# Windowed attention and a gated MLP on one core: probabilities times values by blocks of 64 queries, one piece of PE work for one pair's product and the next pair's scores, both heads in one instruction

## The chip, the core and the metric

The kernel runs on one core of a Trainium2 chip. The metric is the time of one execution in device microseconds. It is 917.48 us at the median of three runs (916.28 to 917.65). A profiled execution of the same kernel took 917.38 us; its span from the first to the last instruction is 915.7 us.

Names of engines: PE is TensorE (PEld its weight loads), DVE is VectorE, ACT is ScalarE, POOL is GpSimd, SP is SyncE, which here only issues DMAs.

## What is computed

Eight batches, eight heads, 576 positions, 64 numbers a head, all fp32. Heads 0 to 3 see the 32 positions up to their own; heads 4 to 7 see every fourth position of the last 128. The eight heads' outputs, side by side, are the 512 columns of x for a gated MLP of 2048 hidden units.

```python
scores = scale * np.matmul(q, k.transpose(0, 1, 3, 2))
rel = pos[:, None] - pos[None, :]
mask_plain = (rel >= 0) & (rel < window)                                       # window = 32
mask_dil = (rel >= 0) & (rel < window * dilation) & (rel % dilation == 0)      # dilation = 4
scores = np.where(masks[None, :, :, :], scores, -1000000000.0)
attn = np.exp(scores - np.max(scores, axis=-1, keepdims=True))
attn = attn / (np.sum(attn, axis=-1, keepdims=True) + 1e-09)
x = np.matmul(attn, v)      # then transposed and reshaped to (8 * 576, 512)
h = x @ w_in
out = (h * (1.0 / (1.0 + np.exp(-1.702 * h)))) @ w_out
```

## The kernel before

**Pairs.** Two heads lie beside each other on 128 partitions, a pair; a batch has four pairs (`c`), 32 in all (`i`). The host sorts the positions of the dilated heads by their remainder modulo 4. A dilated window is then a plain window of 32 neighbours, too, and every query needs only keys of its own block of 32 and of the block before.

**Scores** (L290 to L304). For each block of 32 queries PE multiplies 32 queries by 64 keys, on tiles of 64 x 32 of its array (64 rows for a head, 32 columns for a place among the output partitions). The result of a head is 128 x 5 x 64, `sp`. Batches 0 and 1 have the mask added by PE itself (`masked`, an identity times the mask, L294) and do their scores head by head; from batch 2 on DVE adds the mask (L315 to L318) and both heads come in one piece.

**Softmax** (L306 to L344): maximum, subtraction, exponent, sum, reciprocal, product, for each head by itself where 320 elements a partition are concerned. Then DVE transposes blocks of 32 x 32 into `ct`.

**Spread** (L346 to L365). Eight copies take the blocks of `ct` into `bt`, keys on the partitions, 5 x 32 queries for each group of 128 keys. They are done by ACT or DVE, or by DMAs that SP issues one after the other (batch 1, and pairs 0 and 2 of batch 0, which have the second buffer `bts[1]`, laid into the end of `wol`).

**Product** (L373 to L383). For each group of 128 keys PE multiplies the values (128 x 64) by the probabilities of up to 160 queries, on tiles of 128 x 64, the two heads side by side on the output's partitions. Keys of a group touch queries of the next one, so the pieces overlap and add up in PSUM: 352 columns and 352 columns for the two halves of the queries. The output is x, transposed; ACT takes it out into `xm` (512 positions) and `xr` (the last 64), or in batch 0 ACT and DVE into `xh` and `xl`, its high and low part.

**MLP.** Weights arrive as eight-byte numbers and are decoded on the chip into a high and a low fp32r part (`decode`, L213, 32 pieces `n`, on ACT, DVE and POOL). Group `m0` to `m7` is the 512 first positions of a batch, group `r` the 64 last ones of all eight. A group has 16 ups (`hp`, 12 matmuls of 128 x 512 each, L457) and 16 downs (`acc`, 12 each, L493 to L497), with tanh, gate and split in between. While group m(b) runs on PE, attention of batch b + 1 is worked in between.

**PSUM** has eight banks: `acc0` to `acc3`, `sp0`, `sp1`, `av` and `hp`. Group m0 alternates its ups between `sp1` and `hp` (L451).

**What sets the order.** Nothing is scheduled by hand. Each step is added to a plan (`add`, L44) with its cost on each engine that may do it, an urgency, and the names that it reads and writes. `Plan.ordered` (L64) simulates the engines and gives one order; each engine then runs its instructions in that order, and a waiting instruction holds up all behind it. A step that the plan starts on PE is issued as a whole: for batches from 2 on, scores of both heads are one step (L368), which follows the product of the pair before (`"product"`, L369), and the product is another (L388). In the first 30 us PE's idle time is filled with matmuls that nobody reads (`warm`).

Of the kernel before, what the change touches and what calls it, by code (L numbers as in the profile page):

```python
# [7 lines left out]
F32 = mybir.dt.float32  # L8
# [9 lines left out]
P = 128  # L18
# [8 lines left out]
W = 64  # L27

# [88 lines left out]
def tile_windowed_attention_then_gated_mlp(  # L117
# [50 lines left out]
    zeros, ident = fixed([P, P], BF16, "zeros"), fixed([P, P], BF16, "ident")  # L168
    V.memset(zeros, 0.0)
# [22 lines left out]
    for j in range(2):  # L192
        G.memset(bts[j], 0.0)
# [17 lines left out]
    words = [fixed([P, DM], U32, f"words{j}") for j in range(3)]  # L211

    def decode(n, urgency):  # L213
# [14 lines left out]
        r = n % 3 if n < 5 else n % 5  # L228
        raw, word = cells[r], words[n % 3]
        R, E = f"cell{r}", f"words{n % 3}"  # L230
        taken = {8: ("qk1",), 9: ("qk1", "v1")}.get(n, ())
        freed = () if f < NF - 4 or n % 2 == 0 else ("bt1",)
# [11 lines left out]
        early = ("spread0.3",) if n in (1, 2) else ()  # L244
# [3 lines left out]
        add({DVE: -0.43, ACT: 1.35}, urgency, take_sign, (R,), (R + "l",))  # L248
# [3 lines left out]
            (R + "l",), (E, *freed))  # L252
        add({ACT: 0.62, DVE: -0.42}, urgency, lambda e: copy(e, hi, value), (E,), (key,))
        add({DVE: -0.70, POOL: 1.7}, urgency, lambda e: pair(e, lo, value, f32(hi), ALU.subtract), (E,), (key,))

    spare = [second.bitcast(F32).rearrange("p j n -> p (j n)"), xm.rearrange("p c n -> p (c n)"),
             xr[:, 1:].rearrange("p b c n -> p (b c n)")]

    def attention(b, c, urgency):

        i, dil = b * NC + c, c >= NC // 2
        u = {}
        z = i if b == 0 else 0 if b == 1 else i % 2
        y = (i + 1) % 2 if b < FIRST else 0
        pr, mx, sm, ct, bt = prs[i % 2], mxs[i % 2], sms[i % 2], cts[i % 2], bts[y]
        nq, nv = 2 * S, 2 * QT * D

        def load_qk(e):
            flat = temp([P, nq], F32, "qk", f"qk_{i}") if z == 0 else spare[z - 1][:, 0:nq]
            u["qk"] = flat.rearrange("p (a s) -> p a s", a=2)  # L270
            for rows in (slice(0, D), slice(D, P)) if i == 0 else (slice(0, P),):
                load(u["qk"][rows], qk[i, rows])

        def load_v(e):
            flat = temp([P, nv], F32, "v", f"v_{i}") if z == 0 else spare[z - 1][:, nq:nq + nv]
# [12 lines left out]
        masked, mine = b < FIRST, mask if dil else plain

        def scores(e, heads):  # L290
            for a in heads:
                u["sp", a] = bank([P, QT, W], places[a], f"sp_{i}_{a}")
                if masked:
                    T.matmul(u["sp", a], ident, mine, start=True, stop=False, skip_group_check=True)  # L294
            for t in range(QT):
                for a, j in [(a, j) for a in heads for j in range(min(4, S // 32 - 4 * t))]:
                    g, rows = 4 * t + j, slice(D * a, D * a + D)
                    dst, keys = u["sp", a][32 * j:32 * j + 32, t], u["qk"][rows, 1]
                    for w in (0, 32) if g == 0 else (0,):
                        n = 32 if g == 0 else W  # L300
                        at = max(32 * g - 32, 0)
                        T.matmul(dst[:, w:w + n], u["qk"][rows, 0, 32 * g:32 * g + 32], keys[:, at:at + n],  # L302
                                 start=not masked, stop=True, tile_position=(D * a, 32 * j),
                                 skip_group_check=True)  # L304

        def exponents(a):  # L306

            box, key = pr[:, a], f"{i % 2}{a}"
            held = (places[a],) if masked else ()

            def sp():
                return u["sp", a] if masked else box

            if not masked:
                for n, tiles, cost in ((P, slice(0, QT - 1), 0.35), (D, slice(QT - 1, QT), 0.15)):  # L315
                    add({DVE: cost}, urgency, lambda e, n=n, tiles=tiles: pair(
                        e, box[0:n, tiles], u["sp", a][0:n, tiles], mine[0:n, tiles], ALU.add),
                        (places[a],), (f"pr{key}",))  # L318
            add({DVE: 0.40}, urgency, lambda e: V.tensor_reduce(
                out=mx[:, a], in_=sp(), axis=AX.X, op=ALU.max), (*held, f"pr{key}"), (f"mx{key}",))  # L320
            add({DVE: 0.42}, urgency, lambda e: pair(
                e, box, sp(), mx[:, a, :, None].broadcast_to([P, QT, W]), ALU.subtract),
                (*held, f"mx{key}"), (f"pr{key}",))
            add({ACT: 0.42}, urgency, lambda e: A.activation(box, box, AF.Exp, scale=0.125), (), (f"pr{key}",))  # L324
            add({DVE: 0.40}, urgency, lambda e: V.tensor_reduce(
                out=sm[:, a], in_=box, axis=AX.X, op=ALU.add), (f"pr{key}",), (f"sm{key}",))

        def weights(hs):

            n, heads = hs.stop - hs.start, range(hs.start, hs.stop)  # L330
            sums, probs = [[f"{k}{i % 2}{a}" for a in heads] for k in ("sm", "pr")]
            for a in heads:
                exponents(a)
            add({DVE: -0.075}, urgency, lambda e: V.tensor_scalar(
                out=sm[:, hs], in0=sm[:, hs], scalar1=1.0e-9, scalar2=None, op0=ALU.add), (), sums)
            add({DVE: 0.07 + 0.03 * n}, urgency, lambda e: V.reciprocal(out=sm[:, hs], in_=sm[:, hs]), (), sums)  # L336
            for a in heads:
                add({POOL: 0.73, DVE: -0.48}, urgency, lambda e, a=a: pair(
                    e, pr[:, a], pr[:, a], sm[:, a, :, None].broadcast_to([P, QT, W]), ALU.mult),
                    sums, (f"pr{i % 2}{a}",))  # L340
            for half in (0, 1):
                add({DVE: 0.07 + 0.165 * n}, urgency, lambda e, half=half: V.transpose(  # L342
                    out=ct[:, half, hs], in_=pr[:, hs, :, 32 - 32 * half:64 - 32 * half]),
                    probs, [f"ct{i % 2}{half}{a}" for a in heads])  # L344
# [266 lines left out]
```

## Time and profile before

| what | value |
|---|---|
| median of three runs | 917.48 us |
| profiled execution | 917.38 us |
| its span | 915.7 us |
| granted clock of PE, mean | 0.996 |
| PE busy: `hp_m` (L457), three groups of 512 | 203.1, 199.8, 199.7 us |
| PE busy: scores, `qk` and `second`, 64 x 64 | 20.3 and 13.3 us |
| PE busy: product, 128 x 160, `v` and `second` | 15.6 and 14.3 us |
| ACT busy: copies into `bt`, 32 x 320 | 42.2 us, 468 ns each |
| DVE busy: copies into `bt`, 32 x 320 | 29.2 us, 317 ns each |

In a row of a group stand the line, the engine, the operation, what is written and read, the shapes and the count, and behind the bar the busy time and the mean of one. Matmuls overlap in the pipeline, so the busy times of PE add up to more than the span, and a price of a matmul is read from the distance of two starts. Rows of the timeline give start, busy time, engine, line, operation and count.

### The profile page before, as it was taken

Reading aid. Unit: us, or ns where it says so; the run is one execution under the profiler, and the core shown is the slowest. Engines: PE = TensorE matmul, PEld = TensorE weight load, DVE = VectorE, ACT = ScalarE, POOL = GpSimd, SP = SyncE. Lnnn points to the kernel's source line nnn. Section 1 sums busy time; section 2 is a strip of 40 time slices with the busy share of each in tenths; the row PEclk is TensorE's granted clock in tenths of the full one; section 3 lists DMA queues with packets and bytes.
Section 4 is the critical chain, followed back from the end, with each engine's and each line's share of the span. In section 5 each row is a group of like instructions: output and inputs, shape, how many; then the busy total and the mean of one; then the engine's idle time right before and its main releaser. Section 6 shows DMA issues by size and latency. Waiting matters only on the chain.

```text
span 915.7 us, 16236 instructions
## 1 busy us (share of the span) xinstructions
PE 902.4 (99%) x6738; PEld 726.3 (79%) x6738; DVE 514.1 (56%) x1140; ACT 329.0 (36%) x628; POOL 57.1 (6%) x60
## 2 busy tenths in 40 slices
PE   9899999999999999999999999999999999999997
PEld 4577777888888888888888888888888888888885
DVE  6888896755666546653676275645653433343332
ACT  4888894342433223331434143312431221121111
POOL 3212321000000000000000000000000000000000
PEclk9999999999999999999999999999999999999998
DMA  6645743111112003110221011200100010001002
GB/s 222 229 154 175 272 135 130 63 42 55 50 64 74 23 1 113 42 55 1 87 67 42 15 72 56 67 15 26 62 1 1 1 47 0 1 2 46 1 0 47
DMA packets 25177, 58.54 MB, mean 64 GB/s; under 512 B 6992, under 2 KB 8720, under 8 KB 25104
## 3 DMA queue, kind: packets, MB, share of 16 engines
q1 hardware_dynamic: 25104, 57.50, 19.3%
q8 instruction: 53, 0.87, 0.4%
q14 instruction: 20, 0.16, 0.1%
HBM read 46.14 MB, written 9.44 MB: 61 GB/s over the span
## 4 chain that ended last, share of the span: by engine, by line
PE 92%; ACT 2%; DMA 2%; DVE 2%; SPq 0%; issue 0%; DVEq 0%; ACTq 0%
PE hp_m L457 37%; PE acc_m L493 13%; PE acc_m L497 12%; PE acc_m L494 12%; PE hp_r L457 5%; PE av L381 4%; PE sp L302 3%; PE acc_r L497 2%; PE acc_r L493 2%; PE acc_r L494 2%; DMA qk<-qk_dram 1%; DMA cell<-wo_dram 1%; ACT cell L239 1%; SPq L360 0%; ACT cell L247 0%
## 5 line engine op out<-in xcount | busy, mean ns | idle before, releaser
L468 DVE SCALAR_TENSOR_TENSOR g_m<-g_m,hp_m 128x512 f32<-128x512 f32 x128 | 87.9, 687 | 250.6 <-ACT g_m L465 250.1
L493 PE MATMUL acc_m<-gh,woh 128*128 128x512 f32 x512 | 202.8, 396 | 1.1 <-ACT cell L247 0.4
L457 PE MATMUL hp_m<-xh,wih 128*128 128x512 f32 x512 | 203.1, 397 | 0.5 <-DVE xl L204 0.3
L457 PE MATMUL hp_m<-xh,wil 128*128 128x512 f32 x512 | 199.8, 390 | 0.0
L457 PE MATMUL hp_m<-xl,wih 128*128 128x512 f32 x512 | 199.7, 390 | 0.0
L494 PE MATMUL acc_m<-gh,wol 128*128 128x512 f32 x512 | 199.5, 390 | 0.0
L465 ACT ACTIVATE g_m<-hp_m 128x512 f32<-128x512 f32 x128 | 77.0, 602 | 301.5 <-PE hp_m L457 291.9
L497 PE MATMUL acc_m<-gl,woh 128*128 128x512 f32 x512 | 143.1, 392 | 0.0
L493 PEld LDWEIGHTS acc_m<-gh,woh 128*128 128x128 f32 x512 | 96.1, 188 | 23.7 <-ACT gh L197 1.2
L457 PEld LDWEIGHTS hp_m<-xh,wih 128*128 128x128 f32 x512 | 96.2, 188 | 22.9 <-DVE xl L204 1.0
L457 PEld LDWEIGHTS hp_m<-xl,wih 128*128 128x128 f32 x512 | 96.3, 188 | 20.3
L497 PEld LDWEIGHTS acc_m<-gl,woh 128*128 128x128 f32 x512 | 95.3, 188 | 20.3
L457 PEld LDWEIGHTS hp_m<-xh,wil 128*128 128x128 f32 x512 | 96.3, 188 | 19.0
L494 PEld LDWEIGHTS acc_m<-gh,wol 128*128 128x128 f32 x512 | 96.2, 188 | 19.0
L204 DVE TENSOR_TENSOR gl<-g_m,gh 128x512 fp32r<-128x512 f32 x123 | 87.2, 709 | 13.4 <-ACT gh L197 6.1
L197 ACT ACTIVATE bt<-ct 32x320 f32<-32x320 f32 (+1 forms) x102 | 47.2, 462 | 36.5 <-DVE ct L342 35.1
L324 ACT ACTIVATE pr<-pr 128x320 f32<-128x320 f32 x64 | 29.0, 469 | 66.1 <-DVE pr L204 65.8
L199 DVE CAST gh<-g_m 128x512 fp32r<-128x512 f32 x97 | 42.3, 437 | 9.3 <-PE acc_m L494 0.9
L197 ACT ACTIVATE xm<-av 128x256 f32<-128x256 f32 (+2 forms) x56 | 28.0, 506 | 48.8 <-PE av L381 48.7
L468 DVE SCALAR_TENSOR_TENSOR g_r<-g_r,hp_r 128x512 f32<-128x512 f32 x16 | 11.0, 688 | 54.4 <-ACT g_r L465 54.4
L204 POOL TENSOR_TENSOR pr<-pr,sm 128x320 f32<-128x320 f32 x23 | 18.3, 800 | 335.4 <-DVE sm L336 329.1
L465 ACT ACTIVATE g_r<-hp_r 128x512 f32<-128x512 f32 x16 | 9.6, 598 | 73.4 <-PE hp_r L457 73.4
(104 smaller groups left out, 928.0 us busy)
## 6 DMA issues: line engine op xcount, KB each, us to landing
qk<-qk_dram SPq DMA_DIRECT2D x16, 576.0 KB, 4.1
out_dram<-ost_m SPq DMA_DIRECT2D x32, 256.0 KB, 2.1
second<-qk_dram SPq DMA_DIRECT2D x13, 576.0 KB, 3.9
cell<-wi_dram SPq DMA_DIRECT2D x11, 512.0 KB, 4.7
cell<-wo_dram SPq DMA_DIRECT2D x11, 512.0 KB, 4.5
v<-vp_dram SPq DMA_DIRECT2D x17, 320.0 KB, 2.9
second<-vp_dram SPq DMA_DIRECT2D x13, 320.0 KB, 2.9
second<-wi_dram SPq DMA_DIRECT2D x5, 512.0 KB, 4.3
```

Source lines behind the costliest of these rows:

```text
L197: A.activation(dst, src, AF.Copy, scale=scale)
L199: V.tensor_copy(out=dst, in_=src)
L204: (V if e == DVE else G).tensor_tensor(out=dst, in0=a, in1=b, op=op)
L302: T.matmul(dst[:, w:w + n], u["qk"][rows, 0, 32 * g:32 * g + 32], keys[:, at:at + n], start=not masked, stop=True, tile_position=(D * a, 3 ...
L324: add({ACT: 0.42}, urgency, lambda e: A.activation(box, box, AF.Exp, scale=0.125), (), (f"pr{key}",))
L381: T.matmul(av[D * a:D * a + D, col:col + hi - lo], u["v"][:, a, t], bt[:, lo // 32:hi // 32, a, t], start=m == 0, stop=m == 2, skip_group_ ...
L457: T.matmul(hps[f], st[:, f, c], mv[:, c], start=c == 0 and k == 0, stop=c == NC - 1 and k == 2)
L465: A.activation(self.g32, hps[f], AF.Tanh, scale=0.851)
L468: V.scalar_tensor_tensor(out=self.g32, in0=self.g32, scalar=1.0, in1=hps[f], op0=ALU.add, op1=ALU.mult)
L493: T.matmul(self.acc[j], woh[:, f, cols], gh, start=f == 0, stop=False)
L494: T.matmul(self.acc[j], wol[:, f, cols], gh, start=False, stop=False)
L497: T.matmul(self.acc[j], woh[:, f, P * j:P * j + P], self.g[f][1], start=False, stop=f == NF - 1)
```

## The change

**Product.** The queries go by nine blocks of 64 (`NW`) and the keys by 96 (`KW`): a block needs its own 64 keys and the 32 before it. The host stacks the values accordingly: nine overlapping groups of 96 rows, 432 KB for a pair. `bt` is 96 x 2 x 10 x 64, one buffer for all pairs. The product is nine matmuls of 64 columns for each head, none of which adds to another; the ninth, of the last 64 positions, goes to another bank (`rest`): of the next pair's scores, or in batch 0 to one that otherwise takes the idle matmuls.

**One piece.** From batch 1 on the scores of pair k + 1 and the product of pair k are one step of the plan: on PE the scores come first and the product directly behind them.

**Both heads in one instruction.** Mask, maximum, subtraction, exponent, sum and reciprocal take both heads at once, in all batches. The multiplication by the reciprocal stays apart for each head. The scores of both heads now are one step in all batches.

**Banks.** `sp` is one tile of two banks, `acc` two tiles of two. Group m0 has only `hp` for its ups.

**Spread and loads.** DMAs do the eight copies for batch 1 as before, and two of eight in each pair of batch 0. Queries and keys of pairs 1 and 3, and later of odd pairs, lie in other spare places, and values of odd pairs in `words`. The planner's costs were adapted.

```diff
-    late_bt = wol[:, NF - 4:].bitcast(F32).rearrange("p f n -> p (f n)")[:, 0:10 * QT * 32]
-    bts = [fixed([P, 5, 2, QT, 32], F32, "bt"), late_bt.rearrange("p (j a t n) -> p j a t n", j=5, a=2, t=QT)]
+    bt = fixed([P, 2, NW + 1, D], F32, "bt")
...
-        add({DVE: -0.43, ACT: 1.35}, urgency, take_sign, (R,), (R + "l",))
+        add({DVE: -0.75, ACT: 1.37}, urgency, take_sign, (R,), (R + "l",))
...
+        add({DVE: 0.80}, urgency, lambda e: V.tensor_reduce(out=mx, in_=sp(), axis=AX.X, op=ALU.max),
+            (*held, PR), (MX,))
+        add({DVE: 0.80}, urgency, lambda e: pair(e, pr, sp(), across(mx), ALU.subtract), (*held, MX), (PR,))
+        add({ACT: 0.75}, urgency, lambda e: A.activation(pr, pr, AF.Exp, scale=0.125), (), (PR,))
+        add({DVE: 0.80}, urgency, lambda e: V.tensor_reduce(out=sm, in_=pr, axis=AX.X, op=ALU.add), (PR,), (SM,))
...
+            costs = ({DMA: 82} if NC <= k < FIRST * NC or k < NC and m % 4 == 3 else {ACT: 0.49, DVE: -0.33})
+            add(costs, urgency, work, (f"{CT}.{prev}",), (f"bt.{m}",))
...
-        def product(halves):
-            for hf in halves:
-                parts = ([(0, 0, 160, 0), (1, 0, 160, 128), (2, 0, 32, 256)] if hf == 0 else
-                         [(2, 32, 160, 0), (3, 0, 160, 96), (4, 0, 64, 224)])
...
-                        T.matmul(av[D * a:D * a + D, col:col + hi - lo], u["v"][:, a, t],
-                                 bt[:, lo // 32:hi // 32, a, t],
-                                 start=m == 0, stop=m == 2, skip_group_check=True)
+    def product(k):
+        u = pairs[k]
+        u["av"] = bank([P, GT], "hp" if k < NC and k % 2 else "av", f"av_{k}")
...
+        for m in range(NW):
+            for a in range(2):
+                rows = slice(D * a, D * a + D)
+                dst = u["av"][rows, D * m:D * m + D] if m < NW - 1 else u["rest"][rows]
+                T.matmul(dst, u["v"][0:KW, a, m], bt[0:KW, a, m], start=True, stop=True, skip_group_check=True)
...
+        def work(e):
+            if more:
+                scores(k + 1)
+            product(k)
+
+        add({PE: 2.3 if more else 1.2}, urgency - 1.0e5, work,
+            (lots(k)[1], *(f"bt.{m}" for m in range(8)), *([lots(k + 1)[0]] if more else [])),
+            ("sp", "av"), 1.0)
+        drain_x(k, urgency)
...
-            place = ("sp1", "hp")[f % 2] if self is main[0] else "hp"
+            place = "hp"
```

The order of instructions shows the two places on which most rests. First PE in group m1, before: a product in the middle of a down (`av_1` and `av_0` are its two halves).

```order
L494 MATMUL acc_m_1_1778<-gh_72,wol 128x512
L381 MATMUL av_1_1781<-bt,v_1587 64x128 x2
L381 MATMUL av_1_1781<-bt,v_1587 64x160 x2
L381 MATMUL av_1_1781<-bt,v_1587 64x64 x2
L381 MATMUL av_0_1788<-bt,v_1587 64x160 x4
L381 MATMUL av_0_1788<-bt,v_1587 64x32 x2
L493 MATMUL acc_m_2_1797<-gh_72,woh 128x512
```

Now, on PE in a group of the same kind (m3): the scores of the next pair (L332, 38 matmuls) with the product (L401) directly behind them, between two matmuls of an up.

```order
L509 MATMUL hp_m_2_3615<-xl,wih 128x512
L332 MATMUL sp_3623<-second 32x32 x2
L332 MATMUL sp_3623<-second 32x64 x3
L332 MATMUL sp_3623<-second 32x32 x2
L332 MATMUL sp_3623<-second 32x64 x31
L401 MATMUL av_3662<-bt,v_3155 64x64 x16
L401 MATMUL sp_3623<-bt,v_3155 64x64 x2
L509 MATMUL hp_m_2_3615<-xh,wih 128x512
```

Before, PE went back to full matmuls between the product and the scores; now it goes from the scores' tiles to the product's without one.

The second place is the start on PE. Before, the products of pairs 2 and 3 stood between blocks of the first up, each followed by the block that its x allowed.

```order
L381 MATMUL av_0_545<-wol,xm 64x32 x2
L457 MATMUL hp_m_0_517<-xh,wih 128x512
L457 MATMUL hp_m_0_517<-xh,wil 128x512
L457 MATMUL hp_m_0_517<-xl,wih 128x512
L381 MATMUL av_1_572<-bt,xr 64x128 x2
L381 MATMUL av_1_572<-bt,xr 64x160 x2
L381 MATMUL av_1_572<-bt,xr 64x64 x2
L381 MATMUL av_0_579<-bt,xr 64x160 x4
L381 MATMUL av_0_579<-bt,xr 64x32 x2
L457 MATMUL hp_m_0_517<-xh,wih 128x512
```

Now both products stand together, and the whole first up stands behind them (`idle` is the tile of the idle matmuls, whose bank takes the last 64 positions here).

```order
L619 MATMUL idle<-ident 128x512
L401 MATMUL av_509<-bt,xm 64x64 x16
L401 MATMUL idle<-bt,xm 64x64 x2
L401 MATMUL av_555<-bt,xr 64x64 x16
L401 MATMUL idle<-bt,xr 64x64 x2
L509 MATMUL hp_m_0_594<-xh,wih 128x512
```

No full matmul of group m0 now stands ahead of the product of pair 3.

More of the change, by code (lines that the diff above doesn't have):

```diff
@@ L191, in tile_windowed_attention_then_gated_mlp @@
     V.memset(mask[64:96, 3, 0:16], NEG)
-    for j in range(2):
-        G.memset(bts[j], 0.0)
+    G.memset(bt[0:KW], 0.0)
     def copy(e, dst, src, scale=1.0):
@@ L210, in tile_windowed_attention_then_gated_mlp @@
              second[:, 0], second[:, 1]]
-    words = [fixed([P, DM], U32, f"words{j}") for j in range(3)]
+    words = fixed([P, 3, DM], U32, "words")
     def decode(n, urgency):
@@ new lines, in tile_windowed_attention_then_gated_mlp, with lots, load_qk @@
+    late_v = words.bitcast(F32).rearrange("p j n -> p (j n)")
+    pairs = [{} for _ in range(B * NC)]
+    misc = {}
+    def lots(k):
+        if k < NC:
+            return f"qk{k % 2}", f"v{k}"
+        return ("qk0", "v0") if k < FIRST * NC or k % 2 == 0 else ("qk1", "v1")
+    def load_qk(k):
+        u, place = pairs[k], lots(k)[0]
+        def work(e):
+            if place == "qk0":
+                flat = temp([P, 2 * nq], F32, "qk", f"qk_{k}")
+                both = [flat[:, 0:nq], flat[:, nq:]]
+            else:
+                both = [spare[a][:, nv:nv + nq] for a in range(2)] if k < NC else [spare[0][:, nq * a:nq * a + nq] for a in range(2)]
+            u["q"], u["k"] = both
+            if k and place == "qk0":
+                load(flat.rearrange("p (a s) -> p a s", a=2), qk[k])
+                return
+            for rows in (slice(0, D), slice(D, P)) if k == 0 else (slice(0, P),):
+                for a in range(2):
+                    load(both[a][rows], qk[k, rows, a])
+        add({DMA: 590}, k, work, waits(k), (place,))
@@ new lines, in load_v, with work, waits @@
+    def load_v(k):
+        u, place = pairs[k], lots(k)[1]
+        def work(e):
+            if place == "v0":
+                flat = temp([P, nv], F32, "v", f"v_{k}")
+            else:
+                flat = spare[k - 1][:, 0:nv] if k < NC else late_v[:, 0:nv]
+            u["v"] = flat.rearrange("p (a m d) -> p a m d", a=2, m=NW)
+            load(u["v"][0:KW], vp[k])
+        add({DMA: 442}, k, work, waits(k), (place,))
+    def waits(k):
+        if k >= FIRST * NC and k % 2:
+            return [f"w{x}{f}" for x in "io" for f in range(NF - 3, NF)]
+        return ["xh3.0"] if NC <= k < FIRST * NC else []
@@ L499, in add_hi @@
             def add_hi(j):
-                add({PE: 0.454}, 0.0, lambda e: hi(j), (f"wo{f}", f"gh{f % 2}"), (f"acc{j}",))
+                more = (f"acc{j + 1}",) if f == 0 and j % 2 == 0 else ()
+                add({PE: 0.454}, 0.0, lambda e: hi(j), (f"wo{f}", f"gh{f % 2}"), (f"acc{j}", *more))
             def add_lo(j):
@@ L560, in tile_windowed_attention_then_gated_mlp @@
     last[0].down(last[1])
-    idle = {}
     def warm(e):
-        if 0 in main[0].hps:
-            return
-        if not idle:
-            idle["bank"] = bank([P, GT], "sp1", "idle")
-        T.matmul(idle["bank"], zeros, zeros[:, None, :].broadcast_to([P, GT // P, P]), start=True, stop=True)
+        if 0 not in main[0].hps and "sp" not in pairs[NC]:
+            T.matmul(spare_bank()[:, 0], ident, ident[:, None, :].broadcast_to([P, GT // P, P]), start=True, stop=True)
     for work, e in plan.ordered(warm, WARM):
```

290 lines of the change are left out of this document (142 added, 148 removed).

## The prediction, made before the changed kernel had run

> **What bounds the kernel now.** I read the page first (span, busy time of the engines), then the busy time by stretches, then PE's own timeline.
>
> ```profile
> span 915.7 us, 16236 instructions
> PE 902.4 (99%) x6738; PEld 726.3 (79%) x6738; DVE 514.1 (56%) x1140; ACT 329.0 (36%) x628; POOL 57.1 (6%) x60
> ...
> 0.00:41.00 41.00, 36.22 (x484) 21.04 (x485) 30.49 (x100) 24.97 (x48) 13.42 (x22) 0.96 0.63 211
> ...
> 120.00:126.00 6.00, 5.66 (x25) 4.33 (x25) 5.95 (x14) 6.00 (x9) 1.29 (x1) 1.00 0.44 116
> ...
> 245.00:343.00 98.00, 98.00 (x786) 80.12 (x785) 55.86 (x128) 30.88 (x64) 2.98 (x3) 1.00 0.15 49
> ```
>
> The last three give the stretch, its length, the busy time of PE, weight loads, DVE, ACT and POOL, then granted clock, DMA share and GB/s. There are three stages. Up to 41 us batch 0 goes through attention while the first weights are decoded; much of PE's work there is idle matmuls. Up to 144 us PE runs group m0, with DVE and ACT nearly full beside it. Behind that PE alone is full, at clock 1.00: there a microsecond of PE is a microsecond of the whole. So I price the change by what PE spends on attention.
>
> The timeline of PE in group m2 shows a product and the next scores:
>
> ```profile
> 354.76 0.39 PE L457 MATMUL hp_m<-xl,wih 128*128 128x512 f32 x1
> 354.99 0.39 PE L457 MATMUL hp_m<-xh,wih 128*128 128x512 f32 x1
> ...
> 355.44 0.39 PE L457 MATMUL hp_m<-xl,wih 128*128 128x512 f32 x1
> 355.76 1.46 PE L381 MATMUL av<-bt,second 128*64 128x128 f32 x24
> 357.15 0.50 PE L457 MATMUL hp_m<-xh,wih 128*128 128x512 f32 x1
> 357.49 0.39 PE L457 MATMUL hp_m<-xh,wil 128*128 128x512 f32 x1
> ...
> 359.32 0.39 PE L494 MATMUL acc_m<-gh,wol 128*128 128x512 f32 x1
> 359.64 1.00 PE L302 MATMUL sp<-qk 64*32 64x32 f32 x76
> 360.57 0.50 PE L493 MATMUL acc_m<-gh,woh 128*128 128x512 f32 x1
> 360.91 0.40 PE L494 MATMUL acc_m<-gh,wol 128*128 128x512 f32 x1
> ```
>
> Durations overlap, so only starts count. Full matmuls start every 0.227 us. From 355.44 to 357.49 are 2.05 us where two steps would be 0.45: a product costs **1.60**. Scores: 360.91 - 359.32 = 1.59, less 0.45: **1.14**. A pair costs 2.74. Both have the same rims: 0.09 ahead (0.32 instead of 0.227), and behind, a first full matmul that takes 0.34 instead of 0.227, 0.11.
>
> **Product by 64 queries.** Each fp32 matmul stands twice in the trace (24 for 12), and both heads run side by side, so a chunk of queries is two passes. Asked for ever later moments, the timeline begins with the first matmul still running, which gives starts of passes:
>
> ```profile
> 356.03 0.44 PE L381 MATMUL av<-bt,second 128*64 128x160 f32 x4
> 356.17 0.36 PE L381 MATMUL av<-bt,second 128*64 128x160 f32 x4
> 356.30 0.42 PE L381 MATMUL av<-bt,second 128*64 128x64 f32 x6
> 356.36 0.37 PE L381 MATMUL av<-bt,second 128*64 128x64 f32 x4
> 356.42 0.44 PE L381 MATMUL av<-bt,second 128*64 128x160 f32 x4
> ...
> 356.99 0.23 PE L381 MATMUL av<-bt,second 128*64 128x32 f32 x2
> ...
> 360.43 0.22 PE L302 MATMUL sp<-qk 64*32 64x64 f32 x1
> ```
>
> A 160-column pass takes 0.136 us, a 64-column pass 0.057 on the mean (0.115 for the two from 356.30, before rounding). The first two passes, of 128 columns, take 0.27 (355.76 to 356.03), where 0.85 ns a column (0.136 for 160) makes 0.22: 0.05 is the first weight load, which nothing covers. From first to last start a product now takes 356.99 - 355.76 = 1.23. After: 9 blocks make 18 passes, 17 steps of 0.057 and 0.05: 1.02. **0.21 less.** Fewer rows (96, not 128) I price at nothing; no row has 96. Bounds: nothing, or the quarter that rows could give at most, 0.25.
>
> **One piece instead of two.** The rim behind the scores (0.11) and that ahead of the product (0.09) go: **0.20 less.** What takes their place is the change from the scores' tiles (64*32) to the product's (128*64), which no row has. Ahead of a full matmul a drain lies behind the last small start: 360.57 - 360.43 = 0.14 for scores. Bounds: no drain between the two shapes, or that 0.14. I take 0.14, the nearest row, which is in the 1.14 already. By the Trainium skill, TensorEngine Tiling (Array Packing), Key Properties, changing the tiling mode drains the TensorE. By it the sum stays as I have it, and the trace agrees as far as it goes: 0.14 behind scores. Without it 0.14 more a pair would go.
>
> A merged piece is 2.74 - 0.21 - 0.20 = 2.33. From group m1 on there were 24 products and 23 scores: 24 x 1.60 + 23 x 1.14 = 64.6 us. Now 23 merged pieces and one product alone (1.39): 55.0. **9.6 less.** With no drain between shapes 23 x 0.14 = 3.2 more.
>
> **Group m0.** Batch 1 had scores head by head and products in halves:
>
> ```profile
> 68.08 0.39 PE L457 MATMUL hp_m<-xl,wih 128*128 128x512 f32 x1
> 68.39 0.83 PE L381 MATMUL av<-wol,v 128*64 128x128 f32 x12
> ...
> 69.48 0.39 PE L457 MATMUL hp_m<-xh,wil 128*128 128x512 f32 x1
> ...
> 79.96 0.39 PE L494 MATMUL acc_m<-gh,wol 128*128 128x512 f32 x1
> 80.19 0.31 PE L294 MATMUL sp<-mask,ident 128*128 128x320 bf16 x1
> 80.43 0.76 PE L302 MATMUL sp<-qk 64*32 64x32 f32 x38
> ...
> 81.45 0.39 PE L494 MATMUL acc_m<-gh,wol 128*128 128x512 f32 x1
> ```
>
> Half a product costs 1.40 - 0.45 = 0.95, one head's scores 1.49 - 0.45 = 1.04: 3.98 a pair. Four pairs and the first scores of batch 2 (1.14): 17.1. After: two mask matmuls add about 0.3 to a piece (0.24 from 80.19 to 80.43 for one, and part of that is drain). Scores of pair 4 alone 1.4, three merged pieces with masks 2.63 each, one without 2.33: 11.6. **5.5 less on PE.** But at 120 to 126 us DVE is busy 5.95 of 6 and ACT 6.00, decoding weights that PE waits for: if they don't get faster, PE gains nothing. DVE does get lighter:
>
> ```profile
> L342 DVE STREAM_TRANSPOSE ct<-pr 128x320 f32<-128x320 f32 x48 | 22.3, 493 | 0.8
> L204 DVE TENSOR_TENSOR pr<-sp,mask 128x256 f32<-128x256 f32 x24 | 9.3, 417 | 21.6 <-PE sp L302 21.6
> L342 DVE STREAM_TRANSPOSE ct<-pr 128x160 f32<-128x160 f32 x32 | 9.0, 318 | 1.4 <-DMA wol<-ct 1.3
> L204 DVE TENSOR_TENSOR pr<-sp,mask 64x64 f32<-64x64 f32 x24 | 4.3, 205 | 0.0
> ```
>
> From 64 to 256 elements an addition goes from 205 to 417 ns: 1.1 ns an element, 0.13 us fixed. Both heads in one instruction save that on maximum, subtraction, sum and the two small ones, and 4 x 0.318 - 2 x 0.493 = 0.29 on transposes: 0.9 us of DVE for each of the eight pairs of batches 0 and 1, 7 us in all by the end of m0. Two engines share the decoding, so it ends about half of that sooner. I count **3.5**; bounds 0 and 5.5. Group m0 also loses its second bank for hp. The cover is the 12 acc matmuls (2.7 us) between two ups; a gate that is later than that shows as a wait there.
>
> **Start.** PE waits for DVE's last low part of x and then goes on; the second row begins group m1:
>
> ```profile
> 40.77 0.50 PE L457 MATMUL hp_m<-xh,wih 128*128 128x512 f32 x1 [0.28 <-DVE xl L204]
> ...
> 144.30 0.50 PE L457 MATMUL hp_m<-xh,wih 128*128 128x512 f32 x1
> ...
> 15.43 6.55 SPq L360 DMA_DIRECT2D wol<-ct  x8
> ...
> v<-vp_dram SPq DMA_DIRECT2D x17, 320.0 KB, 2.9
> ```
>
> For: DVE has 0.9 us less a pair, and SP, which spent 6.55 us on issuing eight copies for one pair, issues two for each, so decoding's loads come sooner. Against: values are 432 KB instead of 320, one buffer bt makes each spread wait for the product before it, a pair's two heads no longer overlap, and two products stand ahead of the first full matmul, where three blocks of hp_m_0 and one of hp_m_1 ran before xl was done. I take nothing; bounds 3 us gained, 4 lost.
>
> **Sum.** Against the profiled execution, 917.4 us (span 915.7, and 1.7 around it; the median of the runs is 917.5): 917.4 - 9.6 - 3.5 = **904.3 us**.
>
> **Rivals.**
> - *No drain between the shapes*: 904.3 - 3.2 - 0.4 (three masked pieces) = **900.7**. For it: both shapes already run many tiles at once. Against: every change of shape in the trace drains.
> - *Decoding sets m0, or the start is late*: the 9.6 stay, the 3.5 go, up to 4 come: 907.8 to 911.8, say **909**. For it: 6.00 of 6 on ACT. Against: the lighter DVE.
> - *Weight loads come out from behind the passes*; slower. Passes get shorter, and every one needs its own load. A load that nothing covers costs 0.05 (the first one, above). Eighteen of them cost 0.90 instead of 0.05, for 28 products: 24 us, **928**. It would decide from the point where a load outlasts its pass. Against it: the two 64-column passes from 356.30 have their loads between them and still take 0.057. The Trainium skill, TensorE: Matmul & The Clock Gate, What overlaps and what doesn't, has weight loads overlap matmuls only in other row groups, and both heads' tiles take all rows. By that rule each load would stand bare and this rival be the forecast; the same two passes speak against it.
> - *The product waits for its spread*; slower. It now stands behind the next scores in PE's queue, and all full matmuls stand behind it. Between a pair's scores and its product lie at least 52 full matmuls (11.8 us) and the product before it:
>
> ```profile
> 360.64 0.42 DVE L204 TENSOR_TENSOR pr<-sp,mask 128x256 f32<-128x256 f32 x1
> ...
> 369.13 1.31 DVE L199 COPY bt<-ct 32x320 f32<-32x320 f32 x4
> ...
> 372.81 0.96 PE L381 MATMUL av<-bt,v 128*64 128x128 f32 x14
> ```
>
>   Now this chain takes 370.4 - 360.6, 9.8 us, and has 12.2. Whole heads in one step lose overlap, perhaps 1 to 2 us. It decides from about 13 us on; 1 us late in each of 24 pairs would give **928**.
> - *The merge does nothing* (a rim stays inside the piece): 27 x 0.20 = 5.4 back, **909.7**.
>
> **How the numbers follow.** Forecast 0.52 (901.5 to 907), no drain 0.13, decoding or start 0.19, merge without effect 0.07, bare loads 0.04, late product 0.05. The range 897 to 911 takes in the first four but for their outer ends. A measurement here can tell 0.2%, 1.8 us, from no change. Slower by more: the two slower rivals, 0.09, less what of them stays small, so 0.08. Within: 0.02. Faster: 0.90.
>
> **What would show it.** In group m2, the merged piece should push two full matmuls 2.33 us further apart than their steps; the last scores' start and the product's first should lie 0.14 apart; product passes should follow by 0.057, 18 of them. No wait on bt may stand at the product. Group m1 should begin 3.5 us sooner than 144.3, and from there to the end 9.6 us should be gone. The forecast is wrong if passes take 0.1, if PE waits inside pieces, or if m1 begins later than before.

## The result: slower by 1.1%, and the profile after

| | before | after |
|---|---|---|
| median of four runs each | 917.57 us (916.28 to 919.38) | 927.65 us (926.54 to 930.10) |
| ratio, with its 95% interval | | 1.0112 (1.0085 to 1.0139) |
| span of the profiled execution | 915.7 us | 924.8 us |
| mean granted clock of PE | 0.996 | 0.988 |

The forecast was 904.3 us in 897 to 911, so it is wrong by 23 us and in its sign. First the page of the kernel after, and its busy time in the stretches that were shown of before (PE, weight loads, DVE, ACT, POOL; then PE's clock, DMA share, GB/s):

```profile
span 924.8 us, 16833 instructions
PE 893.0 (97%) x7139; PEld 721.5 (78%) x7139; DVE 520.9 (56%) x990; ACT 322.1 (35%) x595; POOL 40.2 (4%) x41
...
0.00:41.00 41.00, 32.17 (x503) 16.70 (x503) 24.31 (x60) 19.03 (x32) 5.06 (x13) 0.92 0.64 187
120.00:126.00 6.00, 5.78 (x26) 4.43 (x25) 5.64 (x12) 6.00 (x10) 1.87 (x2) 1.00 0.69 234
245.00:343.00 98.00, 97.31 (x836) 80.02 (x835) 56.54 (x109) 29.92 (x60) 2.24 (x2) 1.00 0.17 54
```

PE is busy 9.4 us less, and yet the span is 9.1 longer: PE now idles. Two rows say where. Up to 41 us DVE was busy 30.49 and ACT 24.97 us, now 24.31 and 19.03. And from 245 to 343 us, where PE had no gap, it has one of 0.69.

The merged piece is not the cause. PE's timeline in group m2:

```profile
365.54 0.39 PE L509 MATMUL hp_m<-xh,wil 128*128 128x512 f32 x1
365.77 0.39 PE L509 MATMUL hp_m<-xl,wih 128*128 128x512 f32 x1
366.08 1.00 PE L332 MATMUL sp<-second 64*32 64x32 f32 x76
367.01 1.15 PE L401 MATMUL av<-bt,v 96*64 96x64 f32 x32
368.00 0.29 PE L401 MATMUL sp<-bt,v 96*64 96x64 f32 x4
368.21 0.51 PE L509 MATMUL hp_m<-xh,wih 128*128 128x512 f32 x1
368.55 0.40 PE L509 MATMUL hp_m<-xh,wil 128*128 128x512 f32 x1
```

From 365.77 to 368.55 are 2.78 us where two steps would be 0.45: **2.33**, the forecast to the hundredth. From the scores' first start to the product's are 0.93 (0.78 from first to last start of the scores, by the trace's own starts, and 0.146 of drain; forecast 0.14).

The gaps are elsewhere. Waits of PE from 150 us to the end (what waited for what: us in total, times, longest), and the timeline of ACT and PE at the end of group m1's last down:

```profile
PE acc_m L550 <- ACT ost_m L196: 6.9, 10, 0.7
PE acc_m L550 <- DVE ost_m L200: 0.8, 1, 0.8
PE acc_r L550 <- ACT ost_r L196: 0.7, 1, 0.7
```

```profile
259.58 1.73 ACT L196 ACTIVATE ost_m<-acc_m 128x512 f32<-128x512 f32 x3 [0.70 <-PE acc_m L550]
...
260.06 0.39 PE L546 MATMUL acc_m<-gh,woh 128*128 128x512 f32 x1
260.29 0.39 PE L547 MATMUL acc_m<-gh,wol 128*128 128x512 f32 x1
261.36 0.50 PE L550 MATMUL acc_m<-gl,woh 128*128 128x512 f32 x1 [0.69 <-ACT ost_m L196]
261.70 0.40 PE L509 MATMUL hp_m<-xh,wih 128*128 128x512 f32 x1
```

The low matmul of the last accumulator starts 1.07 us behind its neighbour instead of 0.227, and the next step takes 0.34: 0.95 us. It waits for ACT's copy of the *other* accumulator of the same two-bank tile into `ost`. There are 12 such waits.

The other loss is at the start. PE's timeline from the first product on, and three of DVE's rows there (in brackets the idle time ahead and what ended it):

```profile
24.46 1.15 PE L401 MATMUL av<-bt,v 96*64 96x64 f32 x32
...
26.42 7.25 PE L619 MATMUL idle<-ident 128*128 128x512 bf16 x26 [0.69 <-ACT xr L196]
33.60 1.15 PE L401 MATMUL av<-bt,second 96*64 96x64 f32 x32
...
39.54 1.15 PE L401 MATMUL av<-bt,xm 96*64 96x64 f32 x32
...
44.06 0.48 PE L401 MATMUL av<-bt,xr 96*64 96x64 f32 x4 [3.25 <-ACT bt L196]
...
49.35 0.77 PE L509 MATMUL hp_m<-xh,wih 128*128 128x512 f32 x1 [2.43 <-DVE xl L203]
...
53.81 0.40 PE L509 MATMUL hp_m<-xl,wih 128*128 128x512 f32 x1
```

```profile
34.94 0.32 DVE L198 COPY bt<-ct 32x320 f32<-32x320 f32 x1 [2.55 <-PE idle L401]
...
40.85 0.98 DVE L198 COPY bt<-ct 32x320 f32<-32x320 f32 x3 [0.88 <-PE idle L401]
...
47.76 0.83 DVE L203 TENSOR_TENSOR xl<-av,xh 128x384 fp32r<-128x384 f32 x1 [0.79 <-ACT xh L196]
```

Product 0 starts where it did (24.2 before), but the later ones at 33.6, 39.5 and 44.1 instead of 28.5, 32.4 and 36.7 us, and the twelfth up matmul of m0 at 53.8 instead of 41.3. Of these 12.5 us, 8.6 lie ahead of the up matmul that waits for DVE's last low part of x (40.77 before, 49.35 now). The other 3.9 lie behind it: 12 up matmuls stand there now, where 3 stood, and most of them start 0.43 us apart instead of 0.227, at a granted clock of 0.50. In the kernel after:

```profile
49.35:53.33 3.98, 3.98 (x9) 3.12 (x10) 3.64 (x8) 2.91 (x5) 0.00 (x0) 0.50 0.87 254
```

The span splits into three parts by PE's starts of up matmuls, the first twelve counted in their order (end: the start of PE's last matmul):

| us | before | after | difference | forecast |
|---|---|---|---|---|
| start: to the 12th up matmul | 41.3 | 53.8 | +12.5 | 0 |
| m0: from there to m1's first | 103.0 | 98.2 | -4.8 | -3.5 |
| from m1 to the end | 764.2 | 766.4 | +2.2 | -9.6 |

The last line is -9.4 in pieces and +11.6 from waits on the accumulators, as the first experiments show.

### The profile page after: what moved, and what is told of

Read it like the earlier page. It is cut to its first block, busy times and chain, and to the rows that moved or that the text cites. A ratio compares the mean times of both kernels' runs of the same rounds, so it can differ in the third digit from the quotient of the medians.

```text
span 924.8 us, 16833 instructions
## 1 busy us (share of the span) xinstructions
PE 893.0 (97%) x7139; PEld 721.5 (78%) x7139; DVE 520.9 (56%) x990; ACT 322.1 (35%) x595; POOL 40.2 (4%) x41
## 4 chain that ended last, share of the span: by engine, by line
PE 94%; ACT 2%; DMA 2%; DVE 1%; issue 1%; SPq 1%; ACTq 0%
PE hp_m L509 38%; PE acc_m L550 13%; PE acc_m L546 13%; PE acc_m L547 12%; PE hp_r L509 5%; PE av L401 4%; PE sp L332 3%; PE acc_r L550 2%; PE acc_r L546 2%; PE acc_r L547 2%; PE idle L619 1%; DMA qk<-qk_dram 1%; ACT ost_m L196 1%; DMA bt<-ct 0%; PE sp L401 0%
## 5 line engine op out<-in xcount | busy, mean ns | idle before, releaser
L196 ACT ACTIVATE bt<-ct 32x320 f32<-32x320 f32 x110 | 51.6, 469 | 30.1 <-DVE ct L368 28.3
L198 DVE CAST gh<-g_m 128x512 fp32r<-128x512 f32 x105 | 44.8, 427 | 8.8 <-PE acc_m L547 0.5
L196 ACT ACTIVATE xm<-av 128x512 f32<-128x512 f32 (+2 forms) x42 | 22.8, 613 | 53.1 <-PE av L401 53.1
L358 ACT ACTIVATE pr<-pr 128x640 f32<-128x640 f32 x32 | 23.7, 739 | 49.7 <-DVE pr L203 49.6
L198 DVE COPY bt<-ct 32x320 f32<-32x320 f32 x106 | 33.7, 318 | 5.7 <-PE idle L401 3.4
```

What stands on the lines that cost most here:

```text
L196: A.activation(dst, src, AF.Copy, scale=scale)
L198: V.tensor_copy(out=dst, in_=src)
L358: add({ACT: 0.75}, urgency, lambda e: A.activation(pr, pr, AF.Exp, scale=0.125), (), (PR,))
```

## The experiments

Times are medians. The kernel before had 917.3 to 918.4 us beside them. "Stages" are the three parts of the table above, from each run's own profile.

**The accumulators.** e1 changes only the order in the last down of a group, so that no copy of one accumulator of a tile is issued ahead of the other's last matmul:

```diff
-                for j in range(NC):
-                    add_hi(j)
-                    add_lo(j)
-                    add_out(j)
+                for j in range(0, NC, 2):
+                    for part in (add_hi, add_lo, add_out):
+                        part(j)
+                        part(j + 1)
```

> The changed kernel; only the last down of each group is written in another order: the two high matmul pairs of both accumulators of one two-bank tile, then their two low matmuls, then their two drains. Theory A (the accumulators of one tile wait for each other: the low matmul of the second stands behind ACT's read of the first; 12 waits of 0.85 to 0.95 us in the trace of the changed kernel): the 12 waits go, 927.7 - 11 = 916.5 us. Rival (ACT itself is late at the end of a group, and PE would meet it anyway at the first down of the next group): the waits move there and the time stays at 926 to 928.

Measured: 917.28 us, ratio 0.9996 (0.9983 to 1.0010). All 12 waits are gone, none has come up elsewhere behind m1's start, and the stretch that had a gap is full again. Busy time from 245 to 343 us in e1:

```profile
245.00:343.00 98.00, 98.00 (x840) 80.86 (x839) 57.82 (x112) 29.34 (x59) 2.24 (x2) 1.00 0.17 54
```

e4 is the reverse: the kernel before, with `acc` as two tiles of two banks (batch 0's scores share them) and nothing else:

```diff
-                if f == 0:
-                    self.acc[j] = bank([P, GT], f"acc{j}", f"acc_{self.name}_{j}")
+                if f == 0 and j % 2 == 0:
+                    both = bank([P, 2, GT], f"acc{j // 2}", f"acc_{self.name}_{j}")
+                    self.acc[j], self.acc[j + 1] = both[:, 0], both[:, 1]
```

> The kernel before with one part of the change alone: accumulators in two tiles of two banks (and scores of batch 0 in the same tiles). Theory A: PE waits for drains at the end of groups as in the changed kernel, 12 to 18 waits of 0.9 us: 917.5 + 11 to 16, about 929 us. Rival: the pairing alone costs nothing, 917 to 918.

Measured: 934.18 us, ratio 1.0179 (1.0144 to 1.0215), 16 us more. The theory holds; the waits lie at the upper end of the 12 to 18 that were expected. Waits of PE in e4 from 144 us on:

```profile
PE acc_m L503 <- ACT ost_m L197: 8.9, 13, 0.7
PE acc_m L503 <- DVE ost_m L201: 2.4, 3, 0.8
PE acc_r L503 <- ACT ost_r L197: 0.7, 1, 0.7
```

17 waits of 0.95 us are 16.2 us, the measured difference. The copy and the matmul touch different banks, and in the kernel before, with a tile for each bank, the same order has no such wait: the wait is by tile.

**The idle matmuls in the start.** 26 and 18 of them stand ahead of products 1 and 2, planned for an earlier start. e2 issues none behind product 0; e3 has that and e1's order:

```diff
-        if 0 not in main[0].hps and "sp" not in pairs[NC]:
+        if 0 not in main[0].hps and "av" not in pairs[0]:
```

> The changed kernel without idle matmuls behind the first product of batch 0 (44 matmuls that nobody reads are left out). Theory B (idle matmuls, planned for a start that comes 6 us late, stand ahead of products 1 and 2 in PE's queue): product of pair 1 starts at 29 us instead of 33.6, the first full up at 44 to 45 instead of 49.4, group m1 at 148 instead of 152.0 (decoding takes part of it back), 924 us. Rival (loads and copies into bt set the start, and the idle matmuls only fill gaps): products start where they did, 927 to 928; it could be slower by some 2 us as PE's clock goes down without them.

> Both edits of the two runs before in one kernel (the idle matmuls behind the first product are left out). If the two causes are separate, their gains add: 927.7 - 11 - 4 = 912.7 us. If group m0 is set by decoding and not by its start, 916.

Measured: e2 925.14 us (ratio 1.0080, 1.0052 to 1.0108), e3 915.03 (0.9970, 0.9957 to 0.9982): 2.5 us less than after, 2.3 less than e1. In e3 the twelfth up matmul comes 2.2 us sooner than in e1 (53.0 and 55.2). In e2's profile, of its slowest run (927.19 us), it comes no sooner than in after (53.9 and 53.8). There products 1 and 2 start sooner, at 30.6 and 36.1 us, but product 3 does not (44.4), and the granted clock falls. Busy time of after, then of e2, from 20 to 41 us (the column behind POOL is the clock):

```profile
20.00:41.00 21.00, 17.79 (x233) 9.55 (x231) 13.79 (x33) 12.72 (x23) 2.69 (x3) 0.86 0.42 122
```

```profile
20.00:41.00 21.00, 9.64 (x210) 7.71 (x195) 14.07 (x32) 12.76 (x24) 2.68 (x3) 0.60 0.48 142
```

e3's stages are 53.0, 98.3 and 754.8: from m1 on it has nearly the whole forecast (764.2 - 754.8 = 9.4 of 9.6), in m0 more than it (4.7), and it loses 11.7 in the start. The rest is about these 11.7 us. Experiments on e3's start, with the stages that came out:

| label | edit to e3 | start | m0 | rest | time, us |
|---|---|---|---|---|---|
| e3 | | 53.0 | 98.3 | 754.8 | 915.0 |
| e5 | two spread buffers in batch 0 | 51.9 | 98.2 | 754.8 | 914.0 |
| e6 | no DMA copies in batch 0's spread | 49.5 | 100.3 | 755.0 | 913.8 |
| e19 | e5 and e6 | 50.1 | 100.9 | 754.5 | 914.8 |
| e13 | e19, values of pairs 2, 3 loaded later | 52.2 | 105.9 | 754.9 | 922.0 |
| e8 | product 3 out of the bank of `hp` | 48.0 | 110.8 | 754.8 | 922.0 |
| e9 | e13 and e8 | 47.4 | 102.5 | 754.8 | 915.2 |
| e14 | product 0 ahead of scores 3 | 52.5 | 102.7 | 754.4 | 920.9 |
| e15 | e6 and e14 | 49.8 | 100.9 | 754.8 | 915.7 |

```diff
 e5
+    late = wol[:, NF - 4:].rearrange("p f n -> p (f n)")[:, 0:2 * (NW + 1) * D]
+        return int(k < NC and k % 2 == 0)
...
+            dst = late[row:row + 32, j // 2, j % 2] if side(k) else bt[row:row + 32, :, j // 2::2, 32 * (j % 2):32 * (j % 2) + 32]
...
 e6
-            costs = ({DMA: 82} if NC <= k < FIRST * NC or k < NC and m % 4 == 3 else {ACT: 0.49, DVE: -0.33})
+            costs = ({DMA: 82} if NC <= k < FIRST * NC else {ACT: 0.49, DVE: -0.33})
 e8
+        if k == NC - 1:
+            u["av"] = bank([P, 2, GT], "acc0", f"av_{k}")[:, 0]
...
 e13
+        behind = [lots(k)[0]] if 1 < k < NC else []
+        add({DMA: 442}, k, work, [*waits(k), *behind], (place,))
 e14
-        add({PE: 1.1}, urgency - 1.0e5, lambda e: scores(k), (lots(k)[0],), score_banks(k))
+        add({PE: 4.1 if k > 1 else 1.1}, urgency - 1.0e5, lambda e: scores(k), (lots(k)[0],), score_banks(k))
```

> Base: the run with both edits (e3), 915.0 us, in whose profile the last of the 12 up matmuls of m0's first step ended near 53.4 us (before: 44.3). This kernel gives the pairs 0 and 2 of the first batch a spread buffer of their own in the still empty end of wol (there their probabilities are rounded to PE's fp32r format when they are copied), so that no spread waits for the product ahead of it. Theory S (one bt for four pairs sets the pace of the start): the copies of pair 3 no longer wait 1.12 us for product 2, nor those of pair 1 for product 0, first up matmul at 46 to 47 us instead of 48.1, time 913 to 914. Rival (something else sets the pace, bt is only where the wait ends): 914.5 to 915.5.

> Base: e3, 915.0 us. This kernel copies all eight spread pieces of the first batch's pairs on ACT and DVE; none goes by DMA. Theory D (the two DMA pieces of a pair, 3.4 to 3.6 us from issue to landing, come last): product 2 starts at 36 us instead of 38.2, first up matmul at 46 us instead of 48.1, time about 913. Rival (eight copies of 0.33 to 0.49 us more on two engines that are themselves in the chain cost as much as the landing): 915 to 916.

> Base: e3, 915.0 us. This kernel writes product 3 into the first scores bank (acc0), free by then, instead of the one hp bank. Theory H (the start is late because hp is both the bank of products 1 and 3 and the only bank of the up matmuls, so that all 12 of m0's first step stand behind product 3 and its drain): the first 9 up matmuls run before and beside product 3, in PE time that is idle in e3, only 3 are left behind the last drain, the 12 are done at about 49.5 us instead of 53.4, and the time is 911 to 912. Rival (the time is set by when weights are decoded in m0, an earlier start is waited away there): m0 grows by what the start wins, 914 to 915.

> Base: e3, 915.0 us. This kernel has the edits of e5 (two spread buffers), e6 (no DMA pieces) and e8 (hp free), and loads the values of pairs 2 and 3 behind the queries and keys of these pairs instead of ahead of them. If the start's parts add up: scores 2 at about 16 us instead of 18.6, scores 3 done by 21 instead of 25, first 12 up matmuls done at 44 to 46 us instead of 53.4, time 906 to 908, below both kernels by 1%. If the start is bounded by what DVE and ACT have to do in it (softmax, copies, decodes), no order of loads or banks helps beyond e8: 911 to 912.

e5 and e6 won 1.1 and 1.2 us. In e6 the first up matmul starts at 44.9 us (e3: 48.1), sooner than theory D said. e5's time came as theory S said, but not by its path: the first up matmul starts at 47.9 us, not at 46 to 47. e6 shows what the DMA copies cost in the start, 3.5 us. Issues up to 56 us, KB each and us to landing, first after, then before:

```profile
bt<-ct SPq DMA_DIRECT2D x8, 40.0 KB, 3.6
```

```profile
wol<-ct SPq DMA_DIRECT2D x14, 40.0 KB, 1.9
```

The same 40 KB take nearly twice as long. The new `bt` is written in runs of 32 numbers (packets below 512 bytes up to 56 us: 3088, before 629), but that alone does not make a copy slow. The same copies in the same kernel, from 56 to 150 us:

```profile
bt<-ct SPq DMA_DIRECT2D x32, 40.0 KB, 2.0
```

In the start two of the eight land after 1.96 us, too. The six others, after 3.2 to 4.5, have a weight load of 512 KB under way or issued within 1.6 us of them; that these loads hold them up is not shown.

e8 and e9 were misses. In e8 the start got 5.0 us shorter, as theory H said, but m0 12.5 longer. In e9 the start got 5.6 us shorter and m0 4.2 longer.

> e3 with two spread buffers (e5: 914.0), no DMA pieces (e6: 913.8) and the values of pairs 2 and 3 loaded behind their queries and keys; product 3 stays in the hp bank, unlike e9 (915.2). If these parts of the start add up: 910.5 to 912. If m0 takes back what the start wins: 913 to 915.

> Base: e3, 915.0 us. In e3 the spread of pair 0 is done near 19.5 us, but product 0 stands behind scores 3 in PE's queue (queries and keys of pair 3 late, a stop of 2.4 us in which PE waits for nothing but its own code) and starts at 25.5; ACT and DVE stand in order behind its xh and xl. This kernel only tells the planner that scores 2 and 3 take 4.1 us instead of 1.1, and its order then has product 0 ahead of scores 3. Theory P (that order holds up the chain of products): product 0 at 20 to 21 us, product 1 at 26 to 28 (e3: 30.4), first up matmul at 43 to 45 instead of 48.1, time 910 to 912. Rival (what ACT and DVE have to do in the first 48 us sets the pace, wherever product 0 stands): first up matmul at 47 us or later, 914 to 916. If m0 takes it back, the first up matmul is early and m1 still starts at 150 us or later.

> Base: e6 (e3 without DMA pieces in the first batch), 913.8 us, first up matmul at 44.9. The same planner number as in e14. Theory P: product 0 at 20 to 21 us instead of 23.2, first up matmul at 41 to 43, 910 to 912. Rival: 44 to 45 and 913 to 915.

> e3 with the two spread buffers of e5 (914.0) and without DMA pieces as e6 (913.8), loads in the order of e3, the multiplications where the planner puts them. If the two add up: first up matmul at 43 to 44.5, 911.5 to 912.8. If what the start wins is waited away in m0, as in e8 and e13: 913 to 916.

All four came out on the rivals' side or worse. In e14 products 0 and 1 moved to 21.1 and 25.2 us (e3: 25.4 and 30.4) and product 3 stayed (43.0, e3 43.4). Nor is it the loads alone. Scores of pairs 2 and 3 start at 18.4 and 21.0 us in after (before: 13.4 and 16.6), for the queries and keys of pair 2 now take the place of pair 0's and are issued at 6.9 instead of 3.7 us. In e9 and e13, which load values later, these scores start at 14.3 to 14.8 and 17.9 to 18.7; product 3 stays at 42.2 and 43.0 (before: 36.7). So several chains of nearly one length seem to set the start, and no run takes them apart.

And what the start wins, m0 loses, but for e5. e10, e11 and e12 ask whether the decodes take it. They are e8, e3 and before without the sign steps from the third of the 32 pieces of weights on, whose weights then have no sign; the planner plans each anew:

```diff
+        if n < 2:
             add({DVE: -0.75, ACT: 1.37}, urgency, take_sign, (R,), (R + "l",))
```

> Base: e8 (product 3 out of the hp bank), 922.0 us, where the start ended 5 us sooner than in e3 and m0 took it back with 10.8 us of gaps between full matmuls (e3: 3.6). This kernel is e8 without the decodes' sign step from the third weight matrix on (30 steps of 0.75 us on DVE or 1.37 on ACT; those weights have no sign). Theory W (once the start is earlier, m0 waits for weights: the decodes on DVE and ACT end about 8 us ahead of m1 in each of these kernels): the gaps fall to 4 us or less, m1 starts at 148 to 152 us instead of 158.8, time 911 to 915. Rival (the order of PE's queue in m0 or the one hp bank makes the gaps): 918 or more.

> Base: e3, 915.0 us, m1 at 151.2, 3.6 us of gaps in m0. This kernel is e3 without the sign step of the same 30 decodes. If PE's own work and the late start set m0 there (theory W says decodes bind only once the start is earlier), at most the 3.6 us of gaps go: 912 to 914.5. If the decodes already set m0 in e3: 909 or less.

> Control: the kernel before, 917.6 us, without the sign step of the same 30 decodes. Its m0 has 2.9 us of gaps, so 915 to 917.5; if decodes set its m0 too, 912 or less.

Measured: e10 915.09 us where e8 has 921.99, e11 914.81 (e3: 915.03), e12 917.44 (before: 917.33). So lighter decodes win nothing in before or e3, and 6.9 us in e8. Waits of PE from 60 to 150 us in e8, then in e10:

```profile
PE hp_m L515 <- DVE g_m L526: 3.9, 2, 2.1
PE hp_m L515 <- DVE wil L203: 1.3, 3, 0.7
PE hp_m L515 <- ACT wih L196: 1.2, 1, 1.2
```

```profile
PE acc_m L553 <- ACT gh L196: 1.7, 2, 1.4
PE hp_m L516 <- DVE g_m L527: 1.4, 1, 1.4
```

With lighter decodes the waits on `wih` and `wil` go, and the gate comes sooner. But m0 is 103.5 us in e10, still 5.2 more than in e3.

Waits are only half of what e8 loses in m0. Busy time of e3's m0, of e8's, and of e8 from 103 to 106 us:

```profile
52.95:151.23 98.28, 95.70 (x895) 76.61 (x893) 89.83 (x164) 86.69 (x137) 20.90 (x15) 1.00 0.66 197
48.01:158.78 110.77, 101.50 (x893) 80.23 (x894) 92.41 (x170) 90.40 (x147) 19.96 (x16) 0.94 0.61 185
103.00:106.00 3.00, 3.00 (x9) 2.33 (x9) 3.00 (x8) 2.85 (x4) 0.03 (x1) 0.55 0.71 222
```

PE idles 6.7 us more, and for the same matmuls it is busy 5.8 us longer, as the granted clock falls: from 103 to 106 us full matmuls start 0.43 us apart instead of 0.227. The mean clock of m0 falls in e13 (0.97), e9 (0.97), e14 (0.98) and e10 (0.96), too; in e6, e15 and e19 it stays at 1.00, and what they lose there is in the main longer waits.

e16 takes the lost bank by itself: the kernel before, all ups of m0 in `hp`.

```diff
-            place = ("sp1", "hp")[f % 2] if self is main[0] else "hp"
+            place = "hp"
```

> The kernel before, 917.5 us, with one change: m0's up products have the one bank hp instead of two in turn (sp1 and hp). Its planned order then has all 12 up matmuls of m0's first step behind the last product, as the kernel after has, instead of 9 of them between the products. Theory H (the lost second bank costs at the start, and two waits of about 1.2 us in m0): first 12 up matmuls done at 48 to 50 us instead of 44.3, time 921 to 925. Rival (the start is late for what stands ahead of the products, m0 hides the rest): 917 to 919.

Measured: 918.84 us, ratio 1.0024 (1.0009 to 1.0040). In its profile the start is 47.2 instead of 41.3 us, m0 100.7 instead of 103.0. PE's timeline at products 2 and 3 of e16:

```profile
35.78 1.46 PE L381 MATMUL av<-wol,xm 128*64 128x128 f32 x24
39.18 2.54 PE L381 MATMUL av<-bt,xr 128*64 128x128 f32 x24 [1.95 <-DVE xl L204]
43.24 0.79 PE L457 MATMUL hp_m<-xh,wih 128*128 128x512 f32 x1 [1.52 <-DVE xl L204]
```

As in the kernel after, no up matmul stands between the products. (The 44.3 us of the expectations is not the table's 41.3: there ups of two steps alternate, and the table counts the first twelve of either.) The bank alone moves the start by 5.9 us, as theory H said, but the time by 0.24%, some 2 us, on the rival's side, as m0 gives back 2.3.

Last, POOL: until m1 it does 12 of the multiplications by the reciprocal sums in before (9.6 us), and 3 in e3. e17 (on e6) and e18 (on e9) put all of the first two batches there:

```diff
-            add({POOL: 0.73, DVE: -0.48}, urgency, lambda e, a=a: pair(
+            add({POOL: 0.73} if k < FIRST * NC else {POOL: 0.73, DVE: -0.48}, urgency, lambda e, a=a: pair(
```

> Base: e6 (e3 without DMA pieces), 913.8 us, m1 at 149.8. Until m1 the kernel before does 12 of its multiplications by the reciprocal sums on POOL (9.6 us) and has DVE busy 120.0 us, e3 3 of them (2.2 us) and DVE 125.1. This kernel takes all 16 of the first two batches on POOL. Theory Q (DVE's share of softmax, spread and decodes sets start and m0 together, so that no shorter start alone gets m1 ahead of 149.7 us): m1 at 144 to 147, time 908 to 911. Rival (POOL's 0.73 us each, in the chain from sums to product, and its hold on DVE cost what DVE wins; or the order of the chain, not the work, sets m1): 913 to 917.

> Base: e9 (all parts of the start), 915.2 us, first 12 up matmuls done near 47.8, m1 at 149.9. The same 16 multiplications on POOL. Theory Q: m1 at 144 to 147, time 908 to 911. Rival: 913 to 917.

Measured: 921.79 and 927.68 us. m1 does start sooner (148.0 and 146.6; e6 and e9: 149.8 and 149.9), but from there to the end it takes 764.3 and 771.5 us instead of 755.0 and 754.8. The planner puts one more product behind m1's start, 25 instead of 24, and PE then waits for `xh`, `xl` and the gate, 4.5 and 4.0 us together, and in e18 6.4 us for DMA copies into `bt`. Theory Q falls as a remedy.

## Why the prediction was wrong, step by step

- **The merged piece**: right, in its size and in its parts. 2.33 us forecast, 2.33 measured; passes of 0.058 us (0.057), a drain of 0.146 (0.14), no wait on `bt` at the product from m1 on. Stage from m1 on without the accumulators' waits: -9.4, forecast -9.6. By the Trainium skill (TensorEngine Tiling (Array Packing), Key Properties) a change of tiling mode drains the TensorE; the 0.146 us between the two shapes agree. No run has the blocks of 64 or the merging by itself; the parts are read from the trace.
- **The sum's missing term**: the prediction priced products, scores, rims and decodes, and nothing for `acc` becoming two tiles of two banks, though the description of the change named them. That was 12 x 0.95 = 11.4 us by the trace, 10.4 by e1. It is shown from both sides (e1, e4). The step that failed is "there a microsecond of PE is a microsecond of the whole": it held for the work that went, but the change also made PE wait.
- **Start, "I take nothing; bounds 3 us gained, 4 lost"**: failed; it lost 12.5. The prediction listed causes against it, but balanced them against a lighter DVE and earlier loads. Neither came: up to the twelfth up matmul DVE is busy 34.8 us (before 30.7), and up to 56 us SP issues 10 loads of weights (before 12). Each edit by itself: the lost second bank 5.9 us (e16, in the kernel before), the DMA copies 3.5 (e6), one buffer 1.1 (e5). They do not add: e19, the last two together, wins 2.9 and not 4.6, and all that was tried on e3 at once, e9, wins 5.6 of the 11.7. The rest stays unexplained.
- **Group m0, 3.5 less**: the size is right (4.8; e3: 4.7; bounds 0 to 5.5), the reason is not. The prediction had 5.5 less work on PE, and let only 3.5 of it count, as far as a lighter DVE would end the decodes sooner. DVE is not lighter: up to m1 it is busy 124.4 us (before 119.6). Its merged instructions save some 6 us, about as priced, but the planner gives it 13 of the 16 multiplications by the reciprocal sums, before 4. And decodes set m0 neither in before nor in e3: e12 and e11 win nothing with lighter ones. What fell is PE's own work, as the rows below show: busy 5.8 us less, idle 1.0 more. So the 3.5 is close to the result by luck. For the single bank, "The cover is the 12 acc matmuls" didn't quite hold: in e3 PE waits twice for the gate, for 2.0 us together. The bank's larger cost lay in the start, where the prediction had not put it.
- **Rivals**: "decoding or start late" had the late start, with 4 us at most, and the decoding, which did not come. Drain, passes, spread and rim each came out against their rival. None of the rivals held the accumulators.

Busy time of m0, before and after, for the last but one point:

```profile
41.34:144.30 102.96, 101.20 (x846) 78.04 (x845) 88.88 (x191) 88.25 (x146) 25.05 (x21) 1.00 0.58 194
53.81:151.99 98.18, 95.41 (x894) 76.64 (x893) 89.64 (x164) 86.80 (x137) 20.86 (x15) 1.00 0.65 194
```

The waits in e3 from 60 to 150 us, for the same point:

```profile
PE hp_m L509 <- DVE g_m L520: 2.0, 2, 1.0
PE acc_m L546 <- ACT gh L196: 0.6, 2, 0.3
```

**What stays open.** About half of the start's loss, and why m0 takes back most of what a start wins. In e8 lighter decodes give back 7.3 of 12.5 us of m0 (e10), though under a new plan; for e9, e13, e14, e15 and e19 it is known only that PE waits longer or runs at a lower granted clock, and no run says what brings the clock down there. The best versions, e6 (913.82 us, ratio 0.9964, 0.9949 to 0.9979) and e5 (913.96, 0.9957, 0.9940 to 0.9974), beat before by 0.4% and after by 1.5%, 10 us above the forecast.

## What to carry to other kernels

When a change pairs buffers into one tile, look for the place where one half is drained while the other is still written: the wait was by tile, and reordering the issue so that the drain comes last cost nothing here. A bank or buffer that is lost in the steady stage must also be looked for in the start: here it moved the start by 5.9 us (e16), where the stage behind it showed 2.0 us of waits (e3). A shorter start must be measured together with the stage behind it, its waits and its granted clock: here most of it was lost again there. And a term that comes out right in size still needs its reason tested: m0 gained as forecast, but not because of the decodes.

## What was not expected of the hardware

- PE stops ahead of the last of the scores of pair 3 with nothing to wait for that the trace shows, in after and in e1, e2 and e3. PE's timeline of e3:

```profile
20.90 1.37 PE L332 MATMUL sp<-xm,second 64*32 64x32 f32 x75
24.66 0.31 PE L332 MATMUL sp<-xm,second 64*32 64x64 f32 x1 [2.40 <-issue]
```

  In the trace's DMA records a 16 KB packet of the instruction queue begins at 22.32 us and takes 0.91, and PE goes on 1.43 us after it (after: 21.59, 0.96, and 1.42 until 23.97). It looks like PE's own code arriving late, when two pieces of many small matmuls stand close together; that is not shown, as no run took the stop away by itself.
- Passes of 64 columns with 96 rows: 18 of them take 1.046 us from the first start to the last, 0.058 each with the first load taken off; with 128 rows it was 0.057.
- The copies of 40 KB in 128-byte runs land after 2.0 us from 56 to 150 us, no later than before's long runs (1.9), and after 3.6 in the start.
- The granted clock falls in the middle of m0 in e8 and e13, about a microsecond behind a wait of PE (1.8 us in e8): full matmuls then start 0.43 us apart for some 3 us. No run shows that the wait is the cause.
